# Gated linear attention with a soft mixture of experts: guard, rounding and copies of the first blocks on another engine, FP32 gates in the first four units, and a new order of issue

## The chip, the core and the metric

The kernel runs on one NeuronCore of a Trainium2 chip. The metric is the time of one execution on the device, in microseconds (us). TensorE is PE in the profile, VectorE is DVE, ScalarE is ACT, GpSimd is POOL, and SyncE is SP, which issues the DMAs here.

## What is computed

Four sequences (B) of 768 steps with 8 heads (H) of width 48 (D). Each head keeps a 48 x 48 state that is multiplied, row by row, by a complex gate of magnitude at most 0.999, and takes up one outer product of key and value in each step; the output is the query times the real part of the state. The outputs are the tokens (3072 x 384) of a soft mixture of 8 experts with 4 slots each.

```python
mag = np.sqrt(a_re * a_re + a_im * a_im)
scale = np.minimum(mag, 0.999) / (mag + 1e-06)
a_re_n, a_im_n = (a_re * scale, a_im * scale)
for t in range(S):
    new_re = ar * S_re - ai * S_im
    new_im = ar * S_im + ai * S_re
    S_re, S_im = (new_re + kv, new_im)
    y[:, :, t] = np.einsum('bhd,bhde->bhe', q[:, :, t], S_re)
...
logits = x @ phi
d = softmax over tokens, slot_input = d.T @ x
slot_out[e] = np.maximum(slot_input[e] @ w1[e], 0.0) @ w2[e]
out = softmax over slots (logits) @ slot_out
```

## The kernel before, in words

**Blocks and units.** The 3072 tokens are 24 blocks of 128 (six to a sequence), three blocks to a unit, eight units. A tile of a unit has 128 tokens as partitions and, for each block, 384 columns (8 heads x 48). Instead of stepping through time, a block is computed as a masked attention: the running product of the gates becomes a running sum of logarithms of magnitudes and of phases, taken by a matmul with a triangular matrix.

**Steps of a unit.** `gates` (L639 to L667) makes the log magnitudes of a unit in place, in the tile `aat`: a guard that the real part is large enough (L644, on ACT, with an accumulated sum `amiss`), `Ln`, `Exp`, the ratio of imaginary to real part, its square with a running maximum (`tmax`), `Ln`, a sum, `Exp`, and a `min` (L660). Unit 0 is done in two groups (block 0, then blocks 1 and 2), each other unit in one. L665 copies the result to a high part in F32R on ACT, and L667 makes the low part, the rest, on DVE. `arctan` (L674) gives the phases, with another table of ACT.

**Steps of a block.** `phase` (L676 to L701) adds up the phases on PE (`up`, L685), rounds them to whole turns on ACT by adding a large constant (`n`, L688), takes the difference on DVE (`f`, L691), and makes sine and cosine on ACT (`cs`, L696 and L701). L682 is a small step on one partition that hands the last phase of a block to the next. `expo` (L708 to L722) adds up the log magnitudes on PE in two F32R matmuls, high and low part (`lp`, L713), takes `exp` of plus and minus that on ACT (`ee`, L717 and L719), and stores the last row to DRAM (`rows`, L722); `decay` (L726) loads these rows back, turned, as `rt`. `mults` multiplies `ee` by query and key (L733) and by sine and cosine (L738), both on DVE; its product `hat` is what all later steps of the block read. It is made in place over `ee`, so it waits for the `rows` store. `xpose` turns `hat` on PE in four groups of four transposes (`tp`, L750) and copies each to `hT` on ACT (L753). `score` (L758) multiplies them on PE, and DVE masks (`scT`, L762). `attend` (L783, L785) makes the block's output `yb` on PE, and ACT copies it to `yT` (L788). `delta` (L796 to L803) updates the state `st` on PE and DVE. `xform` (L808, L811) and the class `_Moe` then feed the slots, the logits and the shares of the experts. At the end come the experts: `hidden` (L229), `experts` (L259), `combine0` and `combine1` (L288, L298), and the stores (L963). A flag `bad`, made from the guards, is read into a register of each engine (L991) for a fallback.

**Order.** Each step is a generator; a text, `ORDER`, lists about 2,300 names, each of which runs one part of one step (`g` gates, `t` arctan, `p` phase, `e` expo, `m` mults, `x` xpose, `c` score, `a` attend, `D` delta, `d` decay, `la`, `lq`, `lv` loads of gates, query and key, value, `i` the pieces of unit 0's loads, `w` loads of expert weights, `wu` filler matmuls `wp` on a blank tile, L913). `_InOrder` pins the instructions of each engine to that order, so every engine works strictly through its own list, SP too: a DMA whose tile is not free, or whose data are not there, holds up all DMAs behind it. The tiles `aat`, `qkt` and `vt` have two buffers each, so a unit's load waits until the unit two before is done with its tile. Weight chunks go to seven buffers `wx` as they are issued, then to tiles that are no longer needed.

Of the kernel before, what the change touches and what calls it, by code (L numbers as in the profile page):

```python
# [86 lines left out]
class _Moe:  # L87
# [227 lines left out]
    g3 g3 x9 x9 p4 e4 e4 e3 p4 m3 e4 g3 c3 c3 p4 T2 D2 D2 a1 p3 a1 p3 w0 p3 x11 c4 p4 p5 p5 t3 x11 p4 D2 m3 e4 x13 e5 p4 m4 c4
    p5 p5 x13 x15 x15 g3 x10 la2 x10 p6 p6 p6 a1 x12 g3 p5 p5 p5 L3 c5 c5 D2 a2 a2 a2 p7 p7 p7 m5 g4 x12 g4 x14 x14 g4 D3 g3 D3
    f0 f0 m4 p7 l0 l0 m5 l0 e6 e6 e6 x16 x16 lv1 c6 c6 d1 g4 f2 g4 f2 e7 e7 e7 e8 e8 e8 x17 x17 c7 c7 x21 x21 p8 g4 lq1 q0 D3 q0
    q0 s0 D3 x20 x20 g4 x19 x19 p8 D4 p8 a3 a3 g4 x18 x18 T3 x22 w1 D4 e6 m6 e7 p8 p6 p6 p6 lq2 a3 la3 c8 q0 q0 x22 x23 g4 g4 c8
    x23 t4 c10 p8 p8 p8 a4 p7 p7 c9 p7 m6 x24 D4 e8 x27 x27 g5 m7 d2 c9 x24 D5 D5 D4 m8 q0 p9 c10 s0 s0 a4 a4 p9 p9 f1 m7 f1 c11
    c11 x25 x25 L4 a5 a5 g5 x26 x26 c12 g5 p9 g4 e9 e9 e9 p10 f3 e9 f3 c13 a5 m8 c12 x31 g5 e10 e10 e10 c13 x29 g5 p10 p10 x31  # L320
    p10 p11 D5 f4 f4 g5 g5 e11 e11 x34 w2 e11 a6 a6 x28 l1 l1 a6 x29 D6 g5 m9 q1 q1 g5 l1 x28 q1 x32 s0 x34 q1 x30 x30 x32 p11
    p11 T4 s0 s0 c14 p9 p9 p9 x35 x35 p11 D6 D6 x33 c15 c14 a7 c17 p11 p11 t5 p12 g5 e10 c15 a7 q1 p11 p12 m9 x38 x33 c16 la4 D6
# [770 lines left out]
```

## Time and profile before

| what | value |
|---|---|
| median of 3 runs | 299.17 us (298.9 to 299.53) |
| the profiled execution: its time | 298.75 us |
| the profiled execution: its span | 296.9 us |
| granted PE clock, mean of the span | 0.976 |
| PE, DVE, ACT busy | 270.8, 233.1, 230.2 us |
| bytes moved by DMA | 54.86 MB |

The span is what the profiler shows from the first to the last instruction; the time of the same execution is 1.85 us longer. Durations in the profile are of single instructions. A PE that is busy is not a PE at its peak, since matmuls overlap, so its work is better read from the chain of waits, which shows how long a whole group took when PE went from one to the next. FP32 matmuls leave two records each, transposes and F32R matmuls one.

### The profile page before, as it was taken

The numbers are of one execution on the slowest core, as the hardware profiler recorded it, in microseconds if no ns is written. First come the engines' busy times: TensorE is split into PE (matmuls) and PEld (weight loads), VectorE is DVE, ScalarE is ACT, GpSimd is POOL, SyncE is SP. The second block draws the span as 40 slices with busy tenths as digits, with TensorE's granted clock in tenths as the row PEclk, the third lists the DMA queues.
The fourth block names the chain that finished last, engine by engine and source line by source line (L and its number), as shares of the span: only waits on it lengthen the run. The fifth ranks groups of instructions, "written<-read, shape, count | busy, mean of one in ns | idle before, by whom it ended". The sixth has DMA issues, their size and how long they took to land.

```text
span 296.9 us, 6662 instructions
## 1 busy us (share of the span) xinstructions
PE 270.8 (91%) x2714; PEld 214.7 (72%) x2714; DVE 233.1 (79%) x415; ACT 230.2 (78%) x410; POOL 3.0 (1%) x8
## 2 busy tenths in 40 slices
...
GB/s 179 287 191 83 78 109 153 127 170 327 89 277 3 39 187 274 243 45 160 2 31 211 253 52 82 160 3 2 0 103 418 424 424 425 232 393 420 172 383 176
DMA packets 20789, 54.86 MB, mean 185 GB/s; under 512 B 11536, under 2 KB 13456, under 8 KB 16144
## 3 DMA queue, kind: packets, MB, share of 16 engines
...
## 4 chain that ended last, share of the span: by engine, by line
PE 61%; DMA 17%; ACT 10%; DVE 7%; issue 1%; SPq 1%; DVEq 0%; ACTq 0%
DMA rows<-ee 10%; PE sp L758 10%; PE tp L750 9%; PE yb L783 6%; PE db L796 5%; DMA rt<-rows 5%; PE yb L785 4%; PE op L259 4%; PE up L685 4%; PE hp L229 4%; PE xp L808 3%; PE lp L713 2%; DMA aat<-in_aa_dram 2%; PE lg L109 2%; PE ep L277 2%; PE sip L173 2%
## 5 line engine op out<-in xcount | busy, mean ns | idle before, releaser
L753 ACT COPY hT<-tp 96x512 f32<-96x512 f32 x96 | 53.8, 592 | 8.0 <-PE tp L750 7.7
L750 PE MATMUL tp<-cst,hat 128*96 128x128 f32 x384 | 55.3, 277 | 3.7 <-DVE hat L738 3.7
L758 PE MATMUL sp<-hT,hT 96*128 96x128 f32 x384 | 51.7, 279 | 0.3 <-ACT hT L753 0.3
L750 PEld LDWEIGHTS tp<-cst,hat 128*96 128x96 f32 x384 | 42.7, 128 | 12.0 <-issue 3.8
L758 PEld LDWEIGHTS sp<-hT,hT 96*128 96x128 f32 x384 | 46.7, 191 | 2.4 <-ACT hT L753 1.1
L738 DVE TENSOR_TENSOR hat<-ee,cs 128x1536 f32<-128x1536 f32 x24 | 42.0, 1751 | 1.3 <-ACT cs L701 0.7
L783 PE MATMUL yb<-scT,vt 128*48 128x128 f32 x384 | 36.8, 279 | 3.3 <-DVE scT L762 3.2
L762 DVE TENSOR_TENSOR scT<-sp,cst 128x512 f32<-128x512 f32 x48 | 32.4, 683 | 3.1 <-PE sp L758 2.9
L796 PEld LDWEIGHTS db<-vt,hat 128*96 128x96 f32 x320 | 30.7, 167 | 2.4 <-issue 2.0
L785 PE MATMUL yb<-hT,st 96*48 96x128 f32 x320 | 31.3, 272 | 0.0
L796 PE MATMUL db<-vt,hat 128*96 128x48 f32 x320 | 30.9, 247 | 0.0
L783 PEld LDWEIGHTS yb<-scT,vt 128*48 128x48 f32 x384 | 20.8, 122 | 9.4 <-DVE scT L762 4.6
L685 PE MATMUL up<-aat,cst 128*128 128x384 f32 x48 | 21.0, 519 | 5.4 <-issue 3.3
L733 DVE TENSOR_TENSOR ee<-ee,qkt 128x768 f32<-128x768 f32 x24 | 22.8, 952 | 3.7 <-DMA rows<-ee 3.4
L788 ACT COPY yT<-yb 128x512 f32<-128x512 f32 x24 | 14.1, 589 | 10.3 <-PE yb L785 9.8
L913 PE MATMUL wp<-blank 128*128 128x512 f32 x28 | 18.6, 800 | 1.0 <-POOL blank L908 1.0
L785 PEld LDWEIGHTS yb<-hT,st 96*48 96x48 f32 x320 | 19.3, 123 | 0.0
L713 PE MATMUL lp<-w,tri_t 128*128 128x384 f32 x48 | 14.9, 392 | 4.2 <-ACT w L665 2.5
L691 DVE SCALAR_TENSOR_TENSOR f<-n,up 128x384 f32<-128x384 f32 x24 | 13.1, 546 | 4.2 <-ACT n L688 4.2
L650 DVE TENSOR_TENSOR aat<-aat,gt 128x1152 f32<-128x1152 f32 (+2 forms) x9 | 11.0, 1218 | 6.5 <-ACT gt L648 6.4
L688 ACT ACTIVATE n<-up,kb 128x384 f32<-128x384 f32 x24 | 14.2, 590 | 2.4 <-PE up L685 2.4
L701 ACT ACTIVATE cs<-n,kb 128x384 f32<-128x384 f32 x24 | 14.6, 615 | 0.9 <-DVE n L699 0.9
...
## 6 DMA issues: line engine op xcount, KB each, us to landing
...
```

What stands on the lines that cost most here:

```text
L685: PE.matmul(out=up, lhsT=tri_u[par], rhs=ph, start=True, stop=True)
L713: PE.matmul(out=lp, lhsT=tri_r[par], rhs=parts[u][x][:, j], start=x == 0, stop=x == 1)
L733: DVE.tensor_tensor(out=e, in0=e, in1=qkt[u][:, j], op=ALU.mult)
L738: DVE.tensor_tensor(out=x, in0=e.rearrange("p w (h d) -> p w h d", d=D).unsqueeze(3).broadcast_to(sh), in1=cs[g].unsqueeze(1).broadcast_to ...
L750: PE.transpose(out=tp[:, a, :], in_=hat[g][w][:, 4 * hh + a].rearrange("p c d -> p (c d)"), identity=ident)
L753: ACT.copy(out=hT[g, hh, w], in_=tp)
L758: PE.matmul(out=sp[:, a, :], lhsT=hT[g, hh, 1][:, a, :], rhs=hT[g, hh, 0][:, a, :], start=True, stop=True)
L762: DVE.tensor_tensor(out=t, in0=sp, in1=mask[g % 2].unsqueeze(1).broadcast_to([P, 4, P]), op=ALU.mult)
L783: PE.matmul(out=o, lhsT=vt[u][:, j, h, :], rhs=scT[g, hh][:, a, :], start=True, stop=first)
L785: PE.matmul(out=o, lhsT=st[g - 1][:, h, :], rhs=hT[g, hh, 0][:, a, :], start=False, stop=True)
L796: PE.matmul(out=db[:, h, :], lhsT=hat[g][1][:, h].rearrange("p c d -> p (c d)"), rhs=vt[u][:, j, h, :], start=True, stop=True)
L913: PE.matmul(out=wp.rearrange("p (a c) -> p a c", a=4), lhsT=blank, rhs=blank.unsqueeze(1).broadcast_to([P, 4, P]), start=True, stop=True)
```

## The change

Six edits.

1. For units 0 to 3 (`SPLIT = 4`) `gates` ends with the `min`: no high and low part. `expo` sums the log magnitudes of these units in one FP32 matmul straight from `aat`, with the FP32 triangle `tri_l`.
2. The guard of the first three groups (`GUARD_V = 3`: units 0 and 1) is a `tensor_scalar` on DVE with an accumulated minimum `amin`, instead of ACT's `Relu` with a sum. The flag's check at the end takes both.
3. The rounding of the first four blocks (`ROUND_V = 4`) is a `tensor_scalar` on DVE.
4. The copies `hT<-tp` of the first two blocks (`COPY_V = 2`, eight copies) are made on DVE.
5. The tile and the DRAM array of the gates are laid block by block: real and imaginary part of a block lie together.
6. `ORDER` is new from its first line to its last.

```diff
+SPLIT, GUARD_V, ROUND_V, COPY_V = 4, 3, 4, 2
...
-    wu13 wu2 L0 i0 g0 g0 wu12 g0 g0 i4 i3 i2 g1 wu6 g0 g0 wu9 i1 i5 g0 wu0 g1 tr0 g0 g0 g0 wu4 g0 g1 e0 wu10 e0 e0 wu8 T0 t0 g1
+    wu0 L0 wu7 i0 g0 g0 g0 g0 i4 g0 i3 wu5 g1 wu4 la0 g0 wu11 g0 g0 g0 i1 e0 wu1 g1 i8 i2 g1 wu2 g1 e0 e0 T0 t0 p0 g1 wu10 t1 p0
...
-        aat[u] = io.tile([P, 2, UB, HD], F32, name="aat")
+        aat[u] = io.tile([P, UB, 2, HD], F32, name="aat")
...
-        ACT.activation(out=t, in_=ar, func=AF.Relu, scale=-1.0, bias=kb[:, 3:4], accum_out=amiss[:, x : x + 1])
+        if x < GUARD_V:
+            DVE.tensor_scalar(out=t, in0=ar, scalar1=AR_MIN, scalar2=None, op0=ALU.max, op1=ALU.min, accum_out=amin[:, x : x + 1])
+        else:
+            y = x - GUARD_V
+            ACT.activation(out=t, in_=ar, func=AF.Relu, scale=-1.0, bias=kb[:, 3:4], accum_out=amiss[:, y : y + 1])
...
         DVE.scalar_tensor_tensor(out=ar, in0=ar, scalar=W_MAX, in1=t, op0=ALU.min, op1=ALU.subtract)
+        if u < SPLIT:
+            return
...
-        ACT.activation(out=n, in_=up, func=AF.Identity, bias=kb[:, 4:5])
+        if g < ROUND_V:
+            DVE.tensor_scalar(out=n, in0=up, scalar1=MAGIC, scalar2=None, op0=ALU.add)
+        else:
+            ACT.activation(out=n, in_=up, func=AF.Identity, bias=kb[:, 4:5])
...
-        for x in range(2):
-            PE.matmul(out=lp, lhsT=tri_r[par], rhs=parts[u][x][:, j], start=x == 0, stop=x == 1)
+        if u < SPLIT:
+            PE.matmul(out=lp, lhsT=tri_l[par], rhs=aat[u][:, j, 0], start=True, stop=True)
+        else:
+            for x in range(2):
+                PE.matmul(out=lp, lhsT=tri_r[par], rhs=parts[u][x][:, j], start=x == 0, stop=x == 1)
...
-        ACT.copy(out=hT[g, hh, w], in_=tp)
+        if g < COPY_V:
+            DVE.tensor_copy(out=hT[g, hh, w], in_=tp)
+        else:
+            ACT.copy(out=hT[g, hh, w], in_=tp)
...
+        DVE.tensor_reduce(out=t1[:, 5:6], in_=amin, axis=AX.X, op=ALU.min)
+        DVE.tensor_scalar(out=good[:, 4:5], in0=t1[:, 5:6], scalar1=AR_MIN, scalar2=None, op0=ALU.is_gt)
```

Three places of the lists show what moves. The lines of the changed kernel are its own: from `gates` on they are 8 to 21 higher than those of before.

ACT's list, where blocks 1 and 2 of unit 0 get their magnitudes and unit 1 begins (`gt` and `aat` are the gates, `w` the high part, `ee` the exponentials, `hT` the copies, `n` a rounding). Before:

```order
L658 ACTIVATE gt<-aat,kb 128x768
L753 COPY hT_208<-tp 96x512
L644 ACTIVATE gt,amiss<-aat,kb 128x1152
L665 ACTIVATE w_149<-aat 128x768
L646 ACTIVATE aat<-aat 128x1152
L648 ACTIVATE gt<-aat 128x1152
L717 ACTIVATE ee<-lp 128x384 x2
L719 ACTIVATE ee<-lp 128x384 x2
L753 COPY hT_250<-tp 96x512
L753 COPY hT_257<-tp 96x512
L688 ACTIVATE n<-up,kb 128x384
L654 ACTIVATE gt<-gt,kb 128x1152
```

The same place now:

```order
L666 ACTIVATE gt<-aat,kb 128x768
L654 ACTIVATE aat<-aat 128x3x384
L656 ACTIVATE gt<-aat 128x1152
L733 ACTIVATE ee<-lp 128x384
L735 ACTIVATE ee<-lp 128x384
L733 ACTIVATE ee<-lp 128x384
L735 ACTIVATE ee<-lp 128x384
L662 ACTIVATE gt<-gt,kb 128x1152
```

The guard, the high part, three copies and a rounding have left ACT's list between the two `Exp` and `Ln` of the gates.

DVE's list at the same place, from the `min` of blocks 1 and 2 to the second product `hat` (`w` the low part, `gt,tmax` the squares, `scT` a masked score). Before:

```order
L660 SCALAR_TENSOR_TENSOR aat<-aat,gt 128x768
L691 SCALAR_TENSOR_TENSOR f<-n,up 128x384
L682 SCALAR_TENSOR_TENSOR aat<-f,aat 1x384
L667 TENSOR_TENSOR w_150<-aat,w_149 128x768
L650 TENSOR_TENSOR aat<-aat,gt 128x1152
L652 ISA gt,tmax<-aat 128x1152
L652 ISA tmax 128x1
L691 SCALAR_TENSOR_TENSOR f<-n,up 128x384
```

The same place now:

```order
L699 TENSOR_SCALAR n<-up 128x384
L704 SCALAR_TENSOR_TENSOR f<-n,up 128x384
L668 SCALAR_TENSOR_TENSOR aat<-aat,gt 128x2x384
L649 TENSOR_SCALAR gt,amin<-aat 128x1152
L770 COPY hT_219<-tp 96x512
L770 COPY hT_226<-tp 96x512
L692 SCALAR_TENSOR_TENSOR aat<-f,aat 1x384
L770 COPY hT_239<-tp 96x512
L658 TENSOR_TENSOR aat<-aat,gt 128x3x384
L660 ISA gt,tmax<-aat 128x1152
L660 ISA tmax 128x1
L699 TENSOR_SCALAR n<-up 128x384
```

What left ACT stands here: the guard of unit 1, copies and roundings; the low part is gone.

SP's list around the last unit's rows of decays (`rows` the stores to DRAM, `rt` the loads back, `wx`, `aat`, `qkt` and `we` targets of expert weights). Before:

```order
L722 DMA rows_108<-ee 8x48x1 x3
L598 DMA vt<-in_vv_dram 128x1152
L631 DMA wx<-in_w_dram 128x2048 x3
L631 DMA aat<-in_w_dram 128x2048
L631 DMA qkt<-in_w_dram 128x2048
L726 DMA rt<-rows_108 48x24 x2
L631 DMA aat<-in_w_dram 128x2048
```

The same place now:

```order
L738 DMA rows_109<-ee 8x48x1 x2
L635 DMA wx<-in_w_dram 128x2048
L738 DMA rows_109<-ee 8x48x1
L742 DMA rt<-rows_109 48x24 x2
L635 DMA aat<-in_w_dram 128x2048
L635 DMA qkt<-in_w_dram 128x2048
L635 DMA aat<-in_w_dram 128x2048
```

The `rt` loads now stand ahead of the weight loads to `aat` and `qkt`; the other two chunks to `wx` of that group are issued earlier, before the last unit's rows. At the start of SP's list the three pieces of unit 0's gates are now followed by the gates of unit 1, then by the constants and by block 0's query and key; before, block 0's query and key and the constants came ahead of unit 1's gates.

More of the change, by code (lines that the diff above doesn't have):

```diff
@@ L315 @@
[L315 to L322, printed above, removed]
@@ L327 @@
-    p14 p15 p15 p13 c22 q2 p15 D10 f7 f7 p13 la5 c23 d4 D10 c23 L6 s1 g7 s1 l2 s2 m13 m14 a11 a11 D10 p16 p16 p16 p17 e15 x49
-    x49 x48 x48 c25 c25 c24 c24 a11 e15 g7 e15 e15 e16 e16 g7 x52 x52 m14 D11 D11 D11 x55 x55 lv4 g7 g7 x54 x54 D11 e16 p17 p17
-    p17 x53 x53 x56 q2 x56 q2 c27 g7 g7 l3 l3 a12 a12 a12 e17 e17 e17 lq5 c27 c26 c26 g7 T6 f8 t7 f8 D12 s2 x58 x58 x59 x59 s2
-    a13 a13 m15 m15 p17 g7 x57 x57 q2 q2 p18 e16 m16 p18 p16 p18 p19 D12 a13 f10 f10 q3 e17 c29 p18 D12 g7 f9 p16 p17 p16 c29
@@ new lines @@
+    m3 x13 D2 w0 p6 x13 D3 D3 x15 lv1 a2 g3 wu3 p6 L3 m4 x15 x12 p7 tr0 g4 p7 f0 p7 f2 m5 x14 w1 x12 m4 D2 g4 p7 f0 l0 l0 m5 lq1
+    g4 l0 D3 f2 e6 c6 c6 e6 e6 x14 x17 x17 e7 e7 e7 e8 e8 e8 g4 s0 p8 x21 c7 g4 c7 x19 x19 d1 D3 x21 a3 q0 q0 g4 g4 p8 p8 a3 q0
+    a3 q0 e6 la3 p8 m6 x16 x16 x18 x18 g4 x20 x20 T3 c8 p6 p6 p6 e7 e8 D4 c8 x23 lq2 g4 x23 D4 D4 m6 D4 s0 a4 c9 c9 x22 p7 t4 g5
+    q0 c10 p8 D5 x22 x24 p7 p7 a4 x24 x27 x25 x27 x25 c10 p8 p8 D5 m7 p9 q0 s0 L4 m8 x26 e9 a4 m7 e9 f1 f1 e9 c12 m8 p9 p9 g5
@@ new lines @@
+    c11 g5 c11 e10 x26 p9 p10 a5 a5 d2 c12 a5 e10 e10 p10 p10 g5 g5 p10 f4 f4 f3 x31 x31 c13 c13 x29 g5 e11 f3 x29 l1 lq3 a6 e11
+    e11 D5 a6 g5 g5 l1 l1 q1 q1 q1 p11 x35 x35 e9 e10 m9 x28 x28 s0 T4 q1 s0 s0 t5 m10 p11 p11 x30 x30 D6 g5 p11 a6 la4 p9 c14
+    x34 p9 x34 p11 x33 D6 c14 g5 D6 D6 q1 q1 p9 c15 c15 p12 D7 c17 x32 p10 p10 p10 x33 p11 m9 x32 p11 a7 e11 g6 a7 a7 g5 c17 c16
+    c16 D7 D7 m10 L5 m11 g6 p12 p12 D7 p13 g6 e12 e12 x38 x38 a8 a8 a8 lv2 D8 e12 D8 x39 x39 x36 x41 x36 x37 x41 e13 e13 x40 x40
@@ new lines @@
+    p16 p16 p17 c25 c25 a11 e15 c24 c24 x54 g7 g7 g7 g7 x55 x54 p17 x55 p17 e17 e16 e17 a12 a12 x53 a12 lv4 x53 p17 x52 x52 m15
+    g7 g7 c27 e17 x56 x56 c27 c26 D12 D12 c26 g7 l3 q2 T6 x59 x59 t7 x58 x58 l3 l3 a13 a13 f10 f10 p17 q2 f8 f8 f9 x57 x57 e17
+    d5 m15 p18 p18 f9 q2 x61 x61 g7 x60 x60 D11 a13 D12 lq6 q2 p18 p17 D13 c28 p18 m17 s2 p19 s2 x63 p16 p16 q3 p17 p16 la6 c29
+    q3 x63 p19 L7 c28 w3 m16 c29 m16 g7 g7 g8 w4 w5 f11 x62 x62 s2 s2 s2 p19 a14 a14 p19 lv5 x67 f11 D13 c30 x67 s3 e18 e18 e18
@@ L672, in arctan @@
         u, j0, j1 = GROUPS[x]
-        ai = aat[u][:, 1, j0:j1]
+        ai = aat[u][:, j0:j1, 1]
         ACT.activation(out=ai, in_=ai, func=AF.Arctan)
@@ L678, in phase @@
         par = g % 2
-        ph = aat[u][:, 1, j]
+        ph = aat[u][:, j, 1]
         r = slice(FIRST[par], FIRST[par] + 1)
```

66 lines of the change are left out of this document (34 added, 32 removed).

## The prediction

> **What bounds the kernel now.** I read the page's totals first, then busy time by stages, the chain of waits, the groups by shape, and the timeline of the start.
>
> ```profile
> PE 270.8 (91%) x2714; PEld 214.7 (72%) x2714; DVE 233.1 (79%) x415; ACT 230.2 (78%) x410; POOL 3.0 (1%) x8
> ```
>
> Shares of the whole span hide the stages. Busy time by stage (columns: start:end, length, then PE, PEld, DVE, ACT, POOL, the granted PE clock, the DMA share, GB/s):
>
> ```profile
> 0.00:60.00 60.00, 45.56 (x232) 28.03 (x232) 40.76 (x61) 50.15 (x77) 0.41 (x5) 0.91 0.50 149
> 60.00:100.00 40.00, 37.64 (x386) 33.31 (x387) 38.54 (x58) 38.46 (x67) 0.00 (x0) 1.00 0.56 161
> 100.00:220.00 120.00, 120.00 (x1293) 105.73 (x1292) 113.70 (x191) 112.62 (x204) 0.00 (x0) 1.00 0.40 110
> 220.00:250.00 30.00, 28.93 (x353) 25.59 (x350) 20.12 (x49) 15.65 (x35) 1.81 (x1) 1.00 0.99 404
> ...
> 0.00:21.40 21.40, 14.72 (x24) 5.89 (x24) 8.01 (x20) 13.83 (x22) 0.41 (x5) 0.92 0.67 211
> 21.40:58.30 36.90, 29.77 (x204) 21.68 (x205) 31.05 (x40) 34.62 (x53) 0.00 (x0) 0.91 0.42 120
> 58.30:246.40 188.10, 184.12 (x1991) 162.81 (x1991) 172.17 (x289) 165.79 (x300) 1.78 (x1) 1.00 0.51 161
> ```
>
> Three stages. Up to 21.4 us (the first block's product `hat` starts) everything waits for one chain of small steps. From there to 58.3 us (the fourth product starts) ACT is busy 34.62 of 36.90 us and DVE 31.05, while PE's 29.77 still holds fillers (`wp`). From 58.3 to 246.4 us (the last block's `yT`) PE is busy 184.12 of 188.10 us: PE is the bound, with DVE and ACT close behind until 220 us. So a gain must either bring more real PE work in front of the 58 us mark, shorten PE's list behind it, or take out the 3.98 us in which PE stands.
>
> **Part by part: ACT and DVE.** Mean durations by shape:
>
> ```profile
> L665 ACT ACTIVATE w<-aat 128x1152 fp32r<-128x1152 f32 x7 | 8.2, 1168 | 0.0
> L665 ACT ACTIVATE w<-aat 128x768 fp32r<-128x768 f32 x1 | 0.8, 825 | 0.0
> L665 ACT ACTIVATE w<-aat 128x384 fp32r<-128x384 f32 x1 | 0.5, 522 | 0.6 <-DVE aat L660 0.6
> L667 DVE TENSOR_TENSOR w<-aat,w 128x1152 fp32r<-128x1152 f32 x7 | 9.5, 1351 | 0.0
> L667 DVE TENSOR_TENSOR w<-aat,w 128x768 fp32r<-128x768 f32 x1 | 1.0, 959 | 1.1 <-ACT w L665 1.1
> L667 DVE TENSOR_TENSOR w<-aat,w 128x384 fp32r<-128x384 f32 x1 | 0.6, 558 | 0.6 <-ACT w L665 0.6
> L644 ACT ACTIVATE gt<-aat,kb 128x1152 f32<-128x1152 f32 x7 | 8.8, 1261 | 0.6 <-DVE aat L660 0.6
> L644 ACT ACTIVATE gt<-aat,kb 128x768 f32<-128x768 f32 x1 | 0.9, 935 | 1.9 <-DMA aat<-in_aa_dram 1.9
> L644 ACT ACTIVATE gt<-aat,kb 128x384 f32<-128x384 f32 x1 | 0.6, 614 | 2.6 <-DMA aat<-in_aa_dram 2.6
> L688 ACT ACTIVATE n<-up,kb 128x384 f32<-128x384 f32 x24 | 14.2, 590 | 2.4 <-PE up L685 2.4
> L753 ACT COPY hT<-tp 96x512 f32<-96x512 f32 x96 | 53.8, 592 | 8.0 <-PE tp L750 7.7
> L306 DVE COPY os<-o 128x512 f32<-128x512 f32 x6 | 4.1, 689 | 2.1 <-PE o L288 2.0
> L691 DVE SCALAR_TENSOR_TENSOR f<-n,up 128x384 f32<-128x384 f32 x24 | 13.1, 546 | 4.2 <-ACT n L688 4.2
> L699 DVE TENSOR_SCALAR n<-f 128x384 int32<-128x384 int32 x24 | 8.2, 350 | 0.1
> ```
>
> ACT loses the high parts of units 0 to 3 (0.52 + 0.83 + 3 x 1.17 = 4.9 us), three guards (0.61 + 0.94 + 1.26 = 2.8), four roundings (4 x 0.59 = 2.4) and eight copies (8 x 0.59 = 4.7): 14.8 us, nearly all wanted before 100 us.
>
> DVE loses the low parts (0.56 + 0.96 + 3 x 1.35 = 5.6) and gains three things that the trace doesn't show on it. *Copies* `hT<-tp`: nearest is `os<-o`, also 512 columns out of PSUM: 8 x 0.69 = 5.5. *Roundings*: between `n<-f` (0.35) and `f<-n,up` (0.55, which reads PSUM as they do): 1.4 to 2.2, taken 2.2. *Guards*: at least 3 x 0.35 = 1.05 by `n<-f`, at most the two-input rows, 0.56 + 0.96 + 1.35 = 2.9. Like `n<-f` they read one tensor from SBUF; 0.35 against 0.56 at 384 columns suggests half the two-input growth of 0.40 per 384, so 0.35 + 0.55 + 0.75 = 1.65 is taken.
>
> The Trainium skill (VectorE: DVE Perf Modes, The perf-mode tier table) gives FP32 `tensor_scalar` and copy double rate from SBUF, single rate with a PSUM operand, and two-tensor operations single rate. The rows agree so far: 0.35 against 0.56 at 384 columns. If the guard's accumulator output cancels the double rate, which the page leaves open, the guards cost 2.9 and the sum below rises by 1.2 us.
>
> In front of the fourth product DVE's list loses three low parts (2.87) and gains 1.65 + 2.2 + 5.5; net of steps moved over that point (two `scT`, one `f`, one `n` in; two `st` and the cast out: +0.9) it is 7.4 us longer (6.0 to 8.6 by the bounds). DVE has been busy 8.01 + 31.05 = 39.1 us by then, so 46.5 now.
>
> **The start.** Timeline of the first block, and the cast as first reader of the constants:
>
> ```profile
> 0.99 8.92 PE L913 MATMUL wp<-blank 128*128 128x512 f32 x14 [0.99 <-POOL blank L908]
> ...
> 8.29 0.94 ACT L644 ACTIVATE gt<-aat,kb 128x768 f32<-128x768 f32 x1 [1.87 <-DMA aat<-in_aa_dram]
> ...
> 9.22 0.60 ACT L654 ACTIVATE gt<-gt,kb 128x384 f32<-128x384 f32 x1
> ...
> 10.33 0.29 DVE L920 CAST tri_t<-cst 128x256 fp32r<-128x256 f32 x1
> ...
> 11.09 0.56 DVE L660 SCALAR_TENSOR_TENSOR aat<-aat,gt 128x384 f32<-128x384 f32 x1 [0.48 <-ACT gt L658]
> ...
> 13.34 0.49 ACT L717 ACTIVATE ee<-lp 128x384 f32<-128x384 f32 x1 [0.39 <-PE lp L713]
> ...
> 16.50 0.86 PE L685 MATMUL up<-aat,cst 128*128 128x384 f32 x2
> ```
>
> Block 0 waits on ACT behind the second group's guard, which needs data landing at 8.29. So its next DVE step starts only when the `Ln` of L654 ends, at 9.82. Now the `Ln` no longer waits, but the second guard stands on DVE in front of that step, which starts at 8.29 + 0.55 = 8.84: 1.0 earlier. From `aat` at 11.65 to `ee` at 13.34 lie 1.7 us of split and two matmuls; one FP32 matmul as `up` in this stage takes 0.86 and a hop of 0.1: 0.7 earlier. Against it, the constants are queued behind unit 1's gates, 1152 KB, instead of the 384 KB of `qkt`: 768 KB at the stage's 211 GB/s are 3.7 us, at 404 GB/s 1.9, after a landing somewhere before 10.33. They are wanted at 10.65. I take 0.9 of the 1.7 us as lost to them: `hat` of block 0 comes 0.8 earlier (1.7 earlier to 1.7 later).
>
> DVE stood idle 21.40 - 8.01 = 13.4 us before that product. Less the 0.8, and 0.6 of new work that falls there (two guards and a rounding in, a low part and the cast out), 12.0 are left. 12.0 + 46.5 = 58.5 us: DVE reaches its fourth product at 58.7 with almost no other stall, **0.4 us later than now** (2.1 earlier: 0.9 by the start, 1.4 by the price; 3.9 later: 2.5 and 1.2). What ACT gives up, DVE takes.
>
> **PE.** From the chain of waits (start, length, piece):
>
> ```profile
> 101.84 1.01 PE yb L783 x16
> ...
> 106.21 0.65 PE up L685 x2
> ...
> 121.85 0.71 PE lp L713 x4
> 122.56 0.87 PE tp L750 x8
> ...
> 125.19 0.89 PE sp L758 x8
> ...
> 222.90 15.01 DMA rt<-rows
> ```
>
> A block's `lp` costs 0.71 / 2 = 0.355 us in two F32R matmuls and will cost 0.65 in one FP32 matmul, the shape of `up`: +0.295 a block, 3.5 us for twelve, six of them (1.8) behind the mark. In front of the fourth product's transposes PE's list now holds 4 more `tp` (0.44), 4 more `sp` (8 records, 0.89), 16 more `yb` (32 records, 2.0) and one more `up` (0.65): 4.0 us of work that stood behind it. It fits into the first stage, where PE is busy 44.49 us with fillers in it. Behind the mark PE has 4.0 - 1.8 = **2.2 us less**.
>
> Of PE's 3.98 us standing, 2.36 lie in 60 to 100 us, where ACT (38.46 of 40) has now slack and DVE 2.7 us less to do, and 1.07 in 220 to 250 us. There `rt<-rows` takes 15.01 us behind five weight loads that SP issues first; of those, two now go out long before it, one just before and two after it, and the state update need not wait. I take **1.2 us** off (0 to 2.5).
>
> **The end.** The stores fill SP's queue:
>
> ```profile
> 279.60 13.23 SPq L963 DMA_DIRECT2D out_dram<-os  x16
> ```
>
> The flag's register read now stands before the last two stores: at most one slot, 13.23 / 16 = 0.83 us, taken 0.3. Reordered evictions and the block-wise layout of the gates: nothing, beside the chain.
>
> Sum: +0.4 - 2.2 - 1.2 + 0.3 = -2.7 us on the profiled execution's 298.75 us: 296.05. The median of the runs is 0.42 above that execution, so 296.05 + 0.42 = 296.5 us; bounds -2.1 - 2.2 - 2.5 = -6.8 (292.4) and +3.9 - 2.2 + 0.8 = +2.5 (301.7).
>
> **Rivals.** (1) *DVE becomes the bound.* If DVE still stands 5.85 us between its first and fourth product, as now (36.90 - 31.05), the mark is at 12.0 + 46.5 + 5.85 = 64.4, 6.1 late, and the sum +6.1 - 2.2 - 1.2 + 0.3 = +3.0: 302.2 us. For it: eight copies and four roundings now queue in front of `hat` on DVE, so a transpose that is late holds up the products. Against it: ACT, which caused those stalls, is freed. The change loses from 2.9 us of stall on (2.2 + 1.2 - 0.3 - 0.2). 17%.
>
> (2) *The end is set elsewhere.* DMA is at 0.99 of its time from 220 to 250 us. If the loads that free buffers gate the experts, the earlier blocks only wait longer: 299.2 us. Against it: two weight chunks are issued well earlier now. 12%.
>
> (3) *More than counted.* ACT's release takes out nearly all of PE's standing and the mark comes early: towards the lower bound, 293 us. 17%.
>
> (4) *The clock.* It is 0.91 in the first 60 us, 1.00 later. Now five fillers precede the first `lp`, where seven took 8.92 us: they end near 0.99 + 8.92 x 5 / 7 = 7.4, and PE stands until about 11 us. At half clock the first `lp` and `up` cost 0.65 more each, 1.3 us: 297.8 us. 6%. The Trainium skill (TensorE: Matmul & The Clock Gate, Part 1) says that one idle window of about 3.4 us halves the clock; the row's 0.91 fits such windows at the start.
>
> **How the numbers follow.** The forecast has 48%. A measurement here can tell 0.2%, 0.6 us. Faster: 46 of the forecast's 48, all of (3), 5 of (4) and 3 of (2), 71%; same: 8 of (2) and 2 others, 10%; slower: (1) and 2 others, 19%. The range of 292.0 to 300.5 leaves out most of (1) and the far edge of (3); the forecast's own is 294.0 to 299.0.
>
> **What would show it.** Right: the first product near 20.6 us, the fourth between 56.2 and 61.2, ACT with about 10 us of slack before 60 us, DVE over 90% busy from 22 us, PE standing under 3.5 us from there to the last `yT` near 243.5; `lp` at 0.65 a block for units 0 to 3; `rt` of the last unit landing in a few us. Wrong: the fourth product after 61.4 us (rival 1), or the last `yT` 3 us earlier with the span unchanged (rival 2).

## The result, and the profile after

The changed kernel takes 294.88 us (median of 4 runs, 293.33 to 295.45) beside 299.03 us (298.14 to 299.53, 4 runs) for the kernel before: ratio 0.9856, 95% interval 0.9812 to 0.9900. The forecast was 296.5 us. Run again unedited in a later series, the changed kernel took the same, 294.96 us, but the kernel before only 296.06, with executions from 293.2 to 297.2 us: ratio 0.9974 (0.9943 to 1.0004). So in the first series the sign is as forecast; in the second the interval reaches 1, and a gain isn't shown there. The size depends on the kernel before. Ratios and the range of that second series leave disturbed executions out, medians don't, so they need not agree to the last digit.

The profiled execution took 294.93 us, its span is 293.0 us. First the totals:

```profile
PE 272.9 (93%) x2714; PEld 215.3 (73%) x2714; DVE 236.7 (81%) x430; ACT 218.9 (75%) x387; POOL 3.1 (1%) x8
```

Then busy time by stage, cut at the changed kernel's own first product, fourth product and last `yT` (columns as in the prediction):

```profile
0.00:19.05 19.05, 13.97 (x24) 5.58 (x24) 9.15 (x24) 10.83 (x15) 0.41 (x5) 0.91 0.66 210
19.05:56.81 37.76, 32.39 (x220) 24.12 (x222) 37.04 (x54) 28.63 (x42) 0.00 (x0) 0.91 0.47 108
56.81:242.87 186.06, 184.80 (x1979) 161.66 (x1982) 168.59 (x286) 163.56 (x296) 0.81 (x1) 1.00 0.51 167
242.87:293.00 50.13, 41.70 (x496) 23.93 (x493) 21.96 (x69) 15.86 (x37) 1.84 (x3) 0.95 0.77 311
```

The first product starts at 19.05 us instead of 21.40, the fourth at 56.81 instead of 58.20, the last `yT` at 242.87 instead of 246.48; from there to the end it is 50.13 us instead of 50.42. In the second row DVE is busy 37.04 of 37.76 us: from the first to the fourth product it now hardly stands. In the third PE stands 186.06 - 184.80 = 1.26 us, where it stood 3.98 before.

The start, from the timelines (start, length, engine, line, what it waited for):

```profile
3.89 0.55 DVE L649 TENSOR_SCALAR_CACHE_REDUCE gt<-aat 128x384 f32<-128x384 f32 x1 [2.33 <-DMA aat<-in_aa_dram]
...
6.67 0.95 DVE L649 TENSOR_SCALAR_CACHE_REDUCE gt<-aat 128x768 f32<-128x768 f32 x1
...
7.55 0.55 DVE L664 SCALAR_TENSOR_TENSOR aat<-aat,gt 128x384 f32<-128x384 f32 x1
8.78 0.56 DVE L668 SCALAR_TENSOR_TENSOR aat<-aat,gt 128x384 f32<-128x384 f32 x1 [0.68 <-ACT gt L666]
```

```profile
10.57 0.88 PE L726 MATMUL lp<-aat,cst 128*128 128x384 f32 x2 [3.15 <-DMA cst<-in_consts_dram]
```

The second guard (768 columns) starts without a wait, straight behind the step in front of it. The step behind both, L664, starts at 7.55 us, where its counterpart stood at 9.85. Block 0's magnitudes are ready at 8.78 + 0.56 = 9.34, but `lp` waits for the constants until 10.57.

What the new work on DVE costs, by shape:

```profile
L770 DVE COPY hT<-tp 96x512 f32<-96x512 f32 x8 | 5.3, 675 | 0.0
L699 DVE TENSOR_SCALAR n<-up 128x384 f32<-128x384 f32 x4 | 2.2, 554 | 3.5 <-PE up L695 3.5
L649 DVE TENSOR_SCALAR_CACHE_REDUCE gt<-aat 128x1152 f32<-128x1152 f32 x1 | 1.4, 1353 | 0.0
...
L649 DVE TENSOR_SCALAR_CACHE_REDUCE gt<-aat 128x768 f32<-128x768 f32 x1 | 0.9, 947 | 0.0
...
L649 DVE TENSOR_SCALAR_CACHE_REDUCE gt<-aat 128x384 f32<-128x384 f32 x1 | 0.6, 553 | 2.3 <-DMA aat<-in_aa_dram 2.3
```

Copies and roundings cost what was taken; the guards cost 0.55 + 0.95 + 1.35 = 2.85 us, about the upper bound.

PE's list behind the fourth product, from its first transpose to the last `yT`. Before, that transpose stands at 60.09 us, right behind the product:

```profile
60.09 1.49 PE L750 MATMUL tp<-cst,hat 128*96 128x128 f32 x12 [0.72 <-DVE hat L738]
```

```profile
60.09:246.48 186.39, 183.12 (x1985) 162.41 (x1988) 170.38 (x288) 164.00 (x298) 1.81 (x1) 1.00 0.52 162
```

Now it stands at 59.39:

```profile
59.39:242.87 183.48, 182.22 (x1946) 159.59 (x1947) 166.01 (x283) 160.98 (x292) 0.81 (x1) 1.00 0.50 166
```

```profile
L802 PE MATMUL yb<-scT,vt 128*48 128x128 f32 x336 | 32.0, 277 | 0.0
L804 PE MATMUL yb<-hT,st 96*48 96x128 f32 x288 | 28.0, 272 | 0.0
...
L827 PE MATMUL xp<-cst,yT 128*128 128x128 f32 x84 | 12.0, 275 | 0.0
...
L932 PE MATMUL wp<-blank 128*128 128x512 f32 x2 | 1.0, 594 | 0.0
```

The window of before has 352 + 304 records of `yb`, 80 of `xp` and no filler.

So the 3.9 us of span come from: fourth product 1.39 earlier; from it to its first transpose 0.69 longer (2.58 instead of 1.89; PE is busy for all of it, where it was busy for 1.17); PE's work from there 0.90 less; PE standing there 2.0 less (1.26 instead of 3.27); the end 0.29 shorter.

### The profile page after: what moved, and what is told of

Read it like the earlier page. It is cut to its first block, busy times and chain, and to the rows that moved or that the text cites. A ratio compares the mean times of both kernels' runs of the same rounds, so it can differ in the third digit from the quotient of the medians.

```text
span 293.0 us, 6663 instructions
## 1 busy us (share of the span) xinstructions
PE 272.9 (93%) x2714; PEld 215.3 (73%) x2714; DVE 236.7 (81%) x430; ACT 218.9 (75%) x387; POOL 3.1 (1%) x8
## 4 chain that ended last, share of the span: by engine, by line
PE 66%; DVE 16%; DMA 8%; ACT 4%; issue 2%; SPq 1%; DVEq 0%
PE sp L777 12%; PE tp L766 10%; PE yb L802 6%; PE db L815 6%; DMA rows<-ee 6%; PE yb L804 4%; PE op L261 4%; PE hp L231 4%; PE up L695 4%; PE xp L827 3%; DMA cst<-in_consts_dram 3%; DVE hat L754 2%; DVE ee L749 2%; PE lg L111 2%; PE lp L726 2%; PE sip L175 2%
## 5 line engine op out<-in xcount | busy, mean ns | idle before, releaser
L772 ACT COPY hT<-tp 96x512 f32<-96x512 f32 x88 | 49.2, 585 | 9.3 <-PE tp L766 8.9
L766 PE MATMUL tp<-cst,hat 128*96 128x128 f32 x384 | 54.0, 274 | 2.2 <-DVE scT L781 1.1
L777 PEld LDWEIGHTS sp<-hT,hT 96*128 96x128 f32 x384 | 47.9, 195 | 3.8 <-issue 1.6
L766 PEld LDWEIGHTS tp<-cst,hat 128*96 128x96 f32 x384 | 42.1, 127 | 10.3 <-issue 6.1
L815 PEld LDWEIGHTS db<-vt,hat 128*96 128x96 f32 x320 | 31.7, 170 | 1.6 <-issue 0.9
L815 PE MATMUL db<-vt,hat 128*96 128x48 f32 x320 | 32.5, 251 | 0.0
L932 PE MATMUL wp<-blank 128*128 128x512 f32 x28 | 17.7, 766 | 1.0 <-POOL blank L927 1.0
L733 ACT ACTIVATE ee<-lp 128x384 f32<-128x384 f32 x24 | 12.0, 500 | 4.5 <-PE lp L726 3.9
L726 PE MATMUL lp<-aat,cst 128*128 128x384 f32 x24 | 10.1, 506 | 4.5 <-DMA cst<-in_consts_dram 3.1
L695 PEld LDWEIGHTS up<-aat,cst 128*128 128x128 f32 x48 | 7.6, 197 | 8.6 <-ACT ee L735 3.2
```

The lines of the kernel that those rows point to most:

```text
L695: PE.matmul(out=up, lhsT=tri_u[par], rhs=ph, start=True, stop=True)
L726: PE.matmul(out=lp, lhsT=tri_l[par], rhs=aat[u][:, j, 0], start=True, stop=True)
L766: PE.transpose(out=tp[:, a, :], in_=hat[g][w][:, 4 * hh + a].rearrange("p c d -> p (c d)"), identity=ident)
L772: ACT.copy(out=hT[g, hh, w], in_=tp)
L777: PE.matmul(out=sp[:, a, :], lhsT=hT[g, hh, 1][:, a, :], rhs=hT[g, hh, 0][:, a, :], start=True, stop=True)
L815: PE.matmul(out=db[:, h, :], lhsT=hat[g][1][:, h].rearrange("p c d -> p (c d)"), rhs=vt[u][:, j, h, :], start=True, stop=True)
```

## The experiments

One table first, for each profiled execution. The marks are the starts of the first product, the fourth product and the last `yT`, read from the timelines; the ratio is against the kernel before on the same chip.

| kernel | first | fourth | last `yT` | its time, us | ratio (95% interval) |
|---|---|---|---|---|---|
| before | 21.40 | 58.20 | 246.48 | 298.75 | |
| before_again | 21.9 | 58.7 | 245.1 | 297.01 | 0.9993 (0.9966 to 1.0020) |
| changed | 19.05 | 56.81 | 242.87 | 294.93 | 0.9856 (0.9812 to 0.9900) |
| change_again | 19.3 | 57.1 | 243.2 | 295.36 | 0.9974 (0.9943 to 1.0004) |
| edits_old_order | 19.2 | 62.4 | 249.7 | 301.82 | 1.0183 (1.0148 to 1.0217) |
| order_alone | 19.9 | 68.7 | 259.4 | 312.38 | 1.0584 (1.0547 to 1.0621) |
| parts_back | 19.2 | 65.5 | 257.0 | 309.13 | 1.0363 (1.0325 to 1.0402) |
| copies_back | 18.9 | 61.2 | 247.5 | 299.31 | 1.0145 (1.0107 to 1.0183) |
| copies_more | 19.6 | 63.0 | 250.9 | 302.75 | 1.0209 (1.0141 to 1.0278) |
| guards_back | 19.2 | 56.6 | 241.7 | 293.64 | 0.9976 (0.9947 to 1.0004) |
| roundings_back | 19.0 | 58.3 | 242.7 | 295.52 | 1.0026 (0.9999 to 1.0052) |
| layout_back | 19.7 | 57.1 | 243.2 | 295.18 | 1.0005 (0.9968 to 1.0041) |
| constants_first | 19.0 | 58.0 | 243.2 | 294.83 | 0.9895 (0.9865 to 0.9926) |
| fillers_more | 18.8 | 60.1 | 245.9 | 297.23 | 1.0011 (0.9970 to 1.0052) |

From the fourth product to the last `yT` lie 184.4 to 188.3 us in all but two of them (order_alone, parts_back: 190.7 and 191.5), and from there to the end of the span 49.5 to 50.9. Where a version is several us slower, it has lost most of that before its fourth product.

**Edits without order, order without edits.** edits_old_order is the changed kernel with the old text:

```diff
-    wu0 L0 wu7 i0 g0 g0 g0 g0 i4 g0 i3 wu5 g1 wu4 la0 g0 wu11 g0 g0 g0 i1 e0 wu1 g1 i8 i2 g1 wu2 g1 e0 e0 T0 t0 p0 g1 wu10 t1 p0
+    wu13 wu2 L0 i0 g0 g0 wu12 g0 g0 i4 i3 i2 g1 wu6 g0 g0 wu9 i1 i5 g0 wu0 g1 tr0 g0 g0 g0 wu4 g0 g1 e0 wu10 e0 e0 wu8 T0 t0 g1
...
```

> All edits, with the order of issue of before. Theory (the order and the edits need each other: the lists put later PE work in front of the fourth product only in the new order, while FP32 sums add 3.5 us to PE and the copies fill DVE): 297.5 to 301 us, first product 1 to 2 us earlier than the 21.4 us of before, fourth product not before 57.5 us. Rival 'relief': the 14.8 us taken from ACT are the gain, whatever the order: 294 to 296 us.

order_alone is the kernel before with the new text, the cast `tr0` moved ahead of the first `e0`, and high and low part of units 0 to 3 run straight behind the `min`, since the new text has no place for them:

```diff
-        yield "g9"
+        if u >= 4:
+            yield "g9"
...
-        yield "g10"
+        if u >= 4:
+            yield "g10"
```

> The kernel before with the new order of issue alone (the cast of the triangle moved ahead of the first sum, high and low parts made directly behind the min). Theory (order and edits need each other): ACT carries 14.8 us more in lists that were laid out without them, so the fourth product comes after 60 us and the time is 299 to 303 us. Rival 'order': the new order is the gain and the edits are nearly worth nothing: 294 to 296.5 us.

Measured: 301.9 us beside 296.88 of before for the edits in the old order, 314.03 for the order without the edits: a little above the first theory's range and far above the second's. Each of the two is slower than the kernel before. The waits show where. edits_old_order between first and fourth product (engine, line, releaser: us in total, times, longest):

```profile
DVE hT L770 <- PE tp L766: 3.9, 1, 3.9
```

```profile
PE tp L766 <- DVE hat L754: 3.3, 3, 2.9
PE up L695 <- DVE aat L692: 3.1, 1, 3.1
PE yb L802 <- DVE scT L781: 2.5, 2, 2.0
```

A copy now stands on DVE at a place where the old order had put its transpose late. DVE waits for PE, and PE for DVE. order_alone at the same place, and its window from 20 to 60 us:

```profile
DVE f L693 <- ACT n L690: 6.6, 3, 3.4
DVE aat L650 <- ACT gt L648: 2.6, 1, 2.6
```

```profile
20.00:60.00 40.00, 29.65 (x138) 21.91 (x139) 25.24 (x30) 28.61 (x44) 0.00 (x0) 0.70 0.35 99
```

ACT keeps guards, roundings and copies in an order made for an ACT without them, DVE waits 6.6 us for roundings, PE stands, and its granted clock falls to 0.70 in this stretch (0.91 in the changed kernel's first stages). But this run is not the order by itself: the high and low parts stand where the text leaves them, and PE's `lp` waits 3.4 + 1.5 us for them, about as long as in parts_back, the next run, which has the other edits. An order made afresh for the kernel before, with a place for the parts, was not tried.

**The parts.** parts_back undoes edit 1 alone, the cast moved and the parts placed as in order_alone:

```diff
-        if u < SPLIT:
-            PE.matmul(out=lp, lhsT=tri_l[par], rhs=aat[u][:, j, 0], start=True, stop=True)
-        else:
-            for x in range(2):
-                PE.matmul(out=lp, lhsT=tri_r[par], rhs=parts[u][x][:, j], start=x == 0, stop=x == 1)
+        for x in range(2):
+            PE.matmul(out=lp, lhsT=tri_r[par], rhs=parts[u][x][:, j], start=x == 0, stop=x == 1)
```

> The changed kernel with high and low parts in F32R for units 0 to 3 again. Theory (DVE bound in front of the mark, PE behind it): ACT takes 4.9 us and DVE 5.6 us more, 2.9 of them in front of the fourth product, PE 3.5 us less, 1.8 of them behind the mark: fourth product 2 to 3.5 us later, time 295 to 298 us. Rival 'PE bounds all': the 3.5 us of PE come off, 291.5 to 294 us.

Measured: 307.72 us beside 296.88, far more than either theory gave. PE's waits between first and fourth product:

```profile
PE lp L726 <- ACT w L674: 3.1, 2, 2.1
PE up L695 <- ACT ee L732: 2.2, 1, 2.2
PE lp L726 <- DVE w L677: 1.5, 2, 1.0
```

The split lies in the chain of the decays: `lp` waits 3.1 + 1.5 us for the parts. The FP32 matmul costs PE 0.3 us more a block, but without the two steps before it. PE's granted clock is 0.70 from 20 to 60 us here too. How much of the loss is the split itself, how much its place, which here is fixed behind the `min`, and how much the clock, this run does not tell.

**The copies, fewer and more.** copies_back and copies_more change one number:

```diff
-SPLIT, GUARD_V, ROUND_V, COPY_V = 4, 3, 4, 2
+SPLIT, GUARD_V, ROUND_V, COPY_V = 4, 3, 4, 0
```

(and 3 in copies_more).

> The changed kernel with the eight copies of the first two blocks back on ACT. Theory (between first and fourth product DVE is the bound, with 0.7 us of standing, and ACT has 7.7 us to spare there): DVE loses 5.4 us, ACT takes 4.7, the fourth product comes 1 to 4 us earlier than 56.8 us and the time is 292 to 294.5 us. Rival 'place in line': on ACT the copies stand behind gates and table loads, PE gets its operands later, the fourth product comes later than 57.5 us and the time is 296 to 298 us.

> The changed kernel with the copies of the third block on VectorE too (12 instead of 8). Theory (VectorE has no room left): from the first to the fourth product it stands still for 0.7 us and none of that behind the third product, so four copies of 0.60 us net put the fourth product 1.7 to 2.4 us later and the time 1.5 to 2.4 us longer than the changed kernel's, ratio to the kernel before 0.991 to 0.996. Rival (as guards_back showed, VectorE's work and its stalls trade places, and ScalarE's list is what the chain goes through): fourth product and time within 0.7 us of the changed kernel's.

Measured: 300.59 us (before 296.88) without copies on DVE, 303.25 (before 296.06; the changed kernel 294.96 beside it) with twelve. Without copies the direction is the rival's, and the loss exceeds its range. Eight is the number that this order was made for; an order made for none or for twelve was not tried. With none, DVE loses 8 x 0.675 = 5.4 us of work but stands 9.5 us between its first and fourth product, 6.6 of them behind the second (the 2.0 of L658 lies ahead of it):

```profile
DVE aat L658 <- ACT gt L656: 2.3, 2, 2.0
DVE f L704 <- ACT n L701: 2.0, 1, 2.0
DVE aat L664 <- ACT gt L662: 1.9, 1, 1.9
DVE aat L668 <- ACT gt L666: 1.5, 1, 1.5
```

The reason stands in ACT's timeline:

```profile
49.01 0.58 ACT L772 COPY hT<-tp 96x512 f32<-96x512 f32 x1 [1.72 <-PE tp L766]
...
53.75 0.59 ACT L772 COPY hT<-tp 96x512 f32<-96x512 f32 x1
54.21 1.28 ACT L662 ACTIVATE gt<-gt,kb 128x1152 f32<-128x1152 f32 x1
```

A copy waits for its transpose, and `Ln` of the gates (L662), whose input DVE has ready at 50.1 us, stands behind it and the copies after it; in the changed kernel it starts at 49.62 us, here at 54.21. With twelve, the work of DVE rises, PE waits for a copy, and then runs at a lower clock (the third row is the window of 53 to 64 us):

```profile
PE sp L777 <- DVE hT L770: 1.8, 1, 1.8
```

```profile
DVE scT L781 <- PE sp L777: 1.3, 1, 1.3
```

```profile
53.00:64.00 11.00, 8.88 (x50) 7.68 (x50) 8.88 (x15) 6.74 (x10) 0.00 (x0) 0.65 0.69 202
```

My theory of 1.5 to 2.4 us counted DVE's work alone. The fourth product comes 5.9 us later than in change_again: DVE has 2.7 us more to do ahead of it (4 x 0.675) and stands 3.65 us from the first to the fourth product, where it stood 0.7 in the changed kernel. The time is 7.4 us longer. How much of the standing is the clock was not separated.

**Guards and roundings back.**

```diff
-        if x < GUARD_V:
-            DVE.tensor_scalar(out=t, in0=ar, scalar1=AR_MIN, scalar2=None, op0=ALU.max, op1=ALU.min, accum_out=amin[:, x : x + 1])
...
+            y = x
             ACT.activation(out=t, in_=ar, func=AF.Relu, scale=-1.0, bias=kb[:, 3:4], accum_out=amiss[:, y : y + 1])
```

> The changed kernel with the three first guards on ScalarE again. Theory (VectorE is the bound up to the fourth product, so each edit must pay for its own VectorE time): the guards cost VectorE 2.85 us and 0.25 of accumulator reads, 1.43 of it between first and fourth product, where it stands still for only 0.7 us, while ScalarE waits 9 us there. ScalarE takes the third guard at 24 to 25 us in a wait; the fourth product comes 0.7 to 1.4 us earlier, the time 0.5 to 1.4 us shorter than the changed kernel's, ratio 0.981 to 0.984. Rival (what copies_back showed: work taken back to ScalarE comes back as stalls of VectorE): second guard behind ScalarE's list holds the first product, the third one holds Ln and Exp of unit 1: fourth product 0.5 to 2 us later, ratio 0.988 to 0.994.

```diff
-SPLIT, GUARD_V, ROUND_V, COPY_V = 4, 3, 4, 2
+SPLIT, GUARD_V, ROUND_V, COPY_V = 4, 3, 0, 2
```

> The changed kernel with the four first roundings on ScalarE again. VectorE loses 4 x 0.55 us, ScalarE gains 4 x 0.59. Theory (stalls): a rounding on ScalarE stands behind Exp of the decays or Ln and Exp of the gates, and VectorE's difference f, the next in its list, waits for it, as in copies_back, where one such wait took 2.0 us; first product up to 0.3 us later, fourth product 1 to 3 us later, time 1 to 3 us longer than the changed kernel's, ratio 0.989 to 0.996. Rival (work): VectorE is the bound there, 1.6 us less of it between first and fourth product bring the fourth product 0.5 to 1.5 us forward, ratio 0.980 to 0.984.

guards_back: 295.52 us, ratio 0.9976, the same as the changed kernel's second series (0.9974). Both theories fall: no difference is shown (the two ran on different chips). Its window from first to fourth product, the third guard on ACT, and DVE's wait:

```profile
19.20:56.60 37.40, 31.02 (x220) 22.35 (x220) 35.62 (x52) 29.59 (x43) 0.00 (x0) 0.95 0.43 105
```

```profile
23.86 1.26 ACT L649 ACTIVATE gt<-aat,kb 128x1152 f32<-128x1152 f32 x1 [1.03 <-DVE aat L665]
```

```profile
DVE aat L655 <- ACT gt L653: 1.6, 1, 1.6
```

DVE has 1.4 us less to do and stands 1.1 us more. The guard writes `gt`, of which there is one buffer, so it waits for the last reader of unit 0's `gt`, a step of DVE, on either engine (it starts at 23.67 us on DVE, at 23.86 on ACT), and `Ln` and `Exp` wait for it. It is a link of a chain, and a link may lie on either engine if it takes as long.

roundings_back: 296.8 us, ratio 1.0026 (0.9999 to 1.0052). The fourth product is 1.2 us later than in change_again, in the direction of the theory: from first to fourth product DVE waits 2.7 us for roundings,

```profile
DVE f L704 <- ACT n L701: 2.7, 2, 1.5
```

but PE stands only 0.1 us behind the fourth product's transposes instead of 1.3, and the two profiled executions take the same time (295.52 and 295.36). The intervals overlap a little, and the two ran on different chips: about 1% slower at most, and not shown to be slower.

**The start.** layout_back lays the gates as before:

```diff
-        aat[u] = io.tile([P, UB, 2, HD], F32, name="aat")
+        aat[u] = io.tile([P, 2, UB, HD], F32, name="aat")
...
-            lambda: (aat[0][:, 0:1], aa[0][:, 0:1]),
+            lambda: (aat[0][:, :, 0:1], aa[0][:, :, 0:1]),
```

> The changed kernel with the gates laid as before (all real parts of a unit, then all imaginary ones). Theory: the changed kernel's first product starts at 19.05 us instead of 21.40 mostly because the block-wise layout lets block 0's gates land 0.7 us earlier and those of blocks 1 and 2 before the second guard stands on VectorE. With the old layout the first guard starts near 4.6 us instead of 3.9, the second one waits for data until about 8.3, and the first product comes 0.7 to 1.5 us later; VectorE stands still for only 0.7 us from there to the fourth product, so the loss is passed on: 0.7 to 1.5 us slower than the changed kernel, ratio to the kernel before 0.988 to 0.992. Rival: the start has slack elsewhere (first constants, rows), the layout is neutral as the prediction had it: fourth product and time within 0.3 us of the changed kernel's, ratio 0.984 to 0.987.

constants_first moves one name:

```diff
-    wu0 L0 wu7 i0 g0 g0 g0 g0 i4 g0 i3 wu5 g1 wu4 la0 g0 wu11 g0 g0 g0 i1 e0
+    wu0 L0 wu7 i0 g0 g0 g0 g0 i4 g0 i3 wu5 g1 wu4 i1 la0 g0 wu11 g0 g0 g0 e0
```

> The changed kernel with the load of the first constants issued ahead of unit 1's gates instead of behind them. In the changed kernel the first lp stands ready at 9.3 us and waits for the constants until 10.57. Theory: the constants are the last wait of the first product; lp starts near 9.4, the first product 1.0 to 1.2 us earlier, and since VectorE has no idle time behind it, the fourth product and the time come 0.5 to 1.2 us earlier than the changed kernel's, ratio 0.981 to 0.984. Rival: the first product has another wait just behind (the rows store and its landing, the second Arctan), or unit 1's guard now waits for its data: within 0.3 us of the changed kernel, ratio 0.985 to 0.987.

layout_back's two guards:

```profile
4.36 0.55 DVE L649 TENSOR_SCALAR_CACHE_REDUCE gt<-aat 128x384 f32<-128x384 f32 x1 [2.79 <-DMA aat<-in_aa_dram]
...
7.51 0.95 DVE L649 TENSOR_SCALAR_CACHE_REDUCE gt<-aat 128x768 f32<-128x768 f32 x1 [0.29 <-DMA aat<-in_aa_dram]
```

The layout brings the first data 0.47 us earlier, the second guard 0.84, and the first product 0.4 to 0.6; the fourth product is at 57.1 us as in change_again, and the ratios overlap: for the time the rival holds. The layout is a small part of the 2.35 us of the start. constants_first:

```profile
7.61 0.95 DVE L649 TENSOR_SCALAR_CACHE_REDUCE gt<-aat 128x768 f32<-128x768 f32 x1 [0.68 <-DMA aat<-in_aa_dram]
...
10.33 0.91 PE L726 MATMUL lp<-aat,cst 128*128 128x384 f32 x2 [1.90 <-DVE aat L668]
```

The wait for the constants is gone, as expected, and a wait for the second group's gates has come in its place: they now stand behind the constants, and the second guard starts 0.94 us later than in the changed kernel. The first product starts at 19.0 us, as there. So the changed kernel's early second guard (6.67 us) needs both the layout and the constants' late place in the queue. The median of its six runs is the lowest here, 293.19 us, ratio 0.9895; its profiled execution, 294.83 us, was the slowest of the six, so the trace does not show where the rest comes from. Against the changed kernel's two ratios (0.9856 and 0.9974) it is undecided whether it gains.

**The clock.** fillers_more adds six fillers:

```diff
-    for x in range(14):
+    for x in range(20):
         at("wu", warm, x)
...
-    wu4 la0 g0 wu11 g0 g0 g0 i1 e0 wu1 g1 i8 i2 g1 wu2 g1
+    wu4 la0 g0 wu11 wu14 wu15 g0 g0 g0 i1 e0 wu1 g1 i8 i2 g1 wu2 wu16 g1
...
-    x2 x1 lq0 e2 e1 p2 x3 p2
+    x2 x1 lq0 e2 e1 wu17 wu18 p2 x3 p2
...
-    x4 wu9 e2
+    x4 wu9 wu19 e2
```

> The changed kernel with six more fillers: two behind the fifth (ahead of the first lp), one ahead of the first up, two ahead of the third up (TensorE stands 2.55 us there), one near 33 us. Theory (clock): the stretches at half clock before 60 us lengthen transposes, scores and lp that the products wait for by about 1 us each time; kept busy, TensorE has a granted clock of 0.97 or more in the first 60 us instead of 0.91, the fourth product starts 0.5 to 1.5 us earlier and the time is 0.5 to 1.5 us shorter than the changed kernel's. Rival: products and VectorE's list don't hang on TensorE's clock there, or the fillers, 0.86 us each, stand in front of real work: clock up, fourth product and time within 0.4 us or up to 1 us later.

Measured: 296.87 us beside 294.96 of the changed kernel, the fourth product 3 us later. Two windows of the changed kernel and two of this one (the clock is the third number from the end):

```profile
28.20:35.30 7.10, 7.07 (x29) 5.54 (x30) 7.00 (x12) 5.76 (x9) 0.00 (x0) 0.53 0.69 146
36.30:45.00 8.70, 8.44 (x69) 6.19 (x68) 8.38 (x12) 5.92 (x9) 0.00 (x0) 1.00 0.32 29
```

```profile
28.00:36.00 8.00, 6.04 (x32) 3.53 (x32) 7.90 (x12) 6.64 (x10) 0.00 (x0) 1.00 0.73 184
36.70:43.40 6.70, 6.68 (x27) 4.90 (x28) 5.79 (x9) 1.46 (x2) 0.00 (x0) 0.52 0.05 8
```

With the fillers there is no slow stretch from 28 to 35 us, where hardly anything waits for PE, but one at 36.7 to 43.4, where the second block's transposes, the scores and the third block's `lp` are waited for. The recorded rival has a part in it: the added filler near the old one (`wu19`) stands right in front of that `lp`, and the two together hold it up for 2.6 us at half clock, where the one took 0.86. So in this execution the fillers did not keep the clock (0.94 over the first 60 us, against the 0.97 that the theory asked for), and the theory, that a kept clock brings the product forward, is not tested by it. Its twelve runs fall into a group of 294.0 to 295.0 us (mean clock 0.991 to 0.994) and one from 296.4 us up (0.980 to 0.990), which would fit the theory, but only one, of the slower group, was traced. How much of the 3 us is the clock and how much the filler is not shown.

**The two kernels once more.**

> The changed kernel itself once more, unedited, as the measure for the two that run beside it: ratio 0.981 to 0.990. Its fourth product should lie between 56 and 58.5 us: the runs with one edit differ there by the place at which TensorE's clock falls to half (28 to 35 us in the first profile, 37 to 40.6 us with the constants first).

> The kernel before itself once more, unedited: ratio 1.000 within 0.004. Where the changed kernel was run again it took 294.96 us as at first (294.88), but the kernel before took 296 to 297 us there instead of 299.0. Theory: its executions differ by the place at which TensorE's clock falls to half before 60 us; an execution of 295.5 to 297 us has its fourth product 1.5 to 3 us earlier than the first profile's 58.25, at 55 to 57 us, while the stretch from there to the last yT (188.2 us) and the rest (50.4) are the same within 0.5 us. Rival: the difference lies behind the fourth product: TensorE stands less than 3.98 us there, or the loads of the last stage land earlier, and the fourth product is at 58 us again.

The first came out as expected in its mark, at 57.1 us, but not in its ratio. The second settles part of the question why. Windows of before_again, from its fourth product and from that product's first transpose to the last `yT`, and DVE's wait in the last stage:

```profile
58.68:245.09 186.41, 184.20 (x1992) 162.99 (x1993) 172.40 (x290) 165.77 (x301) 1.81 (x1) 1.00 0.50 161
```

```profile
60.57:245.09 184.52, 183.03 (x1985) 162.40 (x1988) 170.51 (x288) 163.88 (x298) 1.81 (x1) 1.00 0.50 162
```

```profile
DVE st L803 <- DMA rt<-rows: 1.0, 1, 1.0
```

My theory, that the clock before 60 us makes the difference, falls: the fourth product is at 58.68 us, not earlier. The rival holds. In this execution of the kernel before PE stands 1.49 us from the first transpose on where it stood 3.27 in the first one: a wait of 1.0 us of `yb` in the last stage is gone, where DVE waits 1.0 us for `rt` instead of 2.5, and `up` waits 0.6 us instead of 1.4 between 60 and 100 us. The changed kernel's standing there is the same in its two executions (1.26 and 1.32), and `rt` is not waited for in either; nearly all of it is one new wait, of a transpose for a masked score between 100 and 220 us. So between these two later executions the change is worth 295.2 - 293.4 = 1.8 us of span: 1.6 from the mark and 0.2 from the standing, while the rest cancels (the two ran on different chips).

## Why the prediction was right, point by point

**The mark (forecast 0.4 us later; measured 1.4 earlier, 1.6 in the repeats).** The step that failed is the start. DVE's work ahead of the fourth product came out at 9.15 + 37.04 = 46.2 us, forecast 46.5, and of the 5.85 us of stalls 0.7 are left, nearly as the sum assumed (0.2); but DVE stands 9.9 us ahead of the first product, not 12.0. Of the forecast's parts there, "1.0 earlier" for L664 was 2.3: the second guard needn't wait for the data that landed at 8.29 before, since they are there by 6.67. The prediction took the landing at 8.29 over from before; layout_back and constants_first show that the layout and the constants' new place in the queue bring it forward, 0.84 and 0.94 us when one of them is undone. The shorter path to `ee` and the wait for the constants cancel about as forecast (+0.7 and -0.9): from L664 to the first product it is 11.50 us, and was 11.55. The layout, put at nothing, is worth about half a us of this.

**The prices on DVE.** Copies 0.675 (taken 0.69), roundings 0.554 (taken 0.55). Guards at the upper bound, 2.85 instead of 1.65. The Trainium skill (VectorE: DVE Perf Modes, The perf-mode tier table) gives FP32 `tensor_scalar` from SBUF double rate; with an accumulator output the rows show the rate of a two-tensor operation, 0.553 us at 384 columns as L668's 0.558 beside it. The other case that the prediction named has come true. Yet DVE's work came to 46.2 us, and not to 46.5 + 1.2: the sum added up whole durations, while a step that waits for nothing starts before the one in front of it has ended (L664 above starts at 7.55 us, the guard in front of it ends at 7.62). In the chain a copy takes 0.60 us and a rounding 0.48; with 18 more instructions on DVE ahead of the mark (78 in the rows above, 60 before), about 0.075 us each, that is 1.4 us by my estimate. Two errors cancelled here, by luck.

**PE's list (forecast -2.2; measured -0.9).** What moves was counted right: 32 records of `yb`, 8 of `sp`, 4 of `tp` and one `up` less behind the transposes. Two things were left out: a filler that now stands behind the mark (`wp` in the rows above, 0.9 us from its start to the next matmul's) and four `xp` that now stand ahead of the last `yT` (0.44). -2.2 + 0.9 + 0.44 = -0.9. Left out too was the way from the fourth product to its first transpose: some of the work moved in front of the transposes stands right there, and PE gets to them 0.7 us later after the product than before.

**PE standing (forecast -1.2, 0 to 2.5; measured -2.0, and -0.2 in the repeats).** The place was right, `rt` of the last unit and 60 to 100 us, where the standing of 2.36 us falls to 0.10; but 1.16 us of new standing came between 100 and 220 us, where PE had not stood at all, and one execution of before had more standing than another, and the sum was built on that one.

**The end (forecast +0.3; measured -0.3 and +0.1).** Nothing that can be told from none.

The sum, -2.7, lies between the two measured pairs (-3.9 and -1.8 of span), and the time, 296.5, is 1.6 above the median. That it came so close is partly luck: against the first pair the mark was missed by 1.8 us one way, and PE's list with the way to the first transpose by 2.0 the other. The prediction also took 0.6 us as what a measurement here can tell; between the series the kernel before moved by 2 to 3 us. Of the signs: fourth product, DVE over 90% busy (98%), PE standing under 3.5, last `yT` near 243.5 and no wait for `rt` came true; the first product came 1.5 us before the forecast, and ACT has 60 - 42.6 = 17.4 us of slack, not 10.

**The rivals.** (1), stalls of DVE between its products, did not come here (0.7 us, where it took 5.85); in copies_more they came, 3.65 us, with the mark at 63.0 and 302.75 us. (2), the end set elsewhere, is out: the end kept its length in every version. (3) was near in the first pair. (4), the clock, shows up in fillers_more and copies_more, though its share there was not separated, not in the first `lp` that the prediction put it on (0.88 us). The first `up`, the other matmul that it named, did take 1.17 us in a stretch at 0.50, but the chain of waits to the first product goes through `lp`, `ee` and `rows`.

Open: why the kernel before took 298 to 299.5 us in the first runs, and 296 to 297 in the median in the later series, on three chips. The traced difference in PE's standing, 1.8 us, is of that size, but it is one execution of each.
